# A spectral filter and an MLP on one core: one semaphore per loaded buffer, other first loads, and a new fixed order

## The chip, the core and the metric

The kernel runs on one core of a Trainium2 chip. The core has a matrix engine (TensorE, "PE" in the profile; its weight loads are "PEld"), VectorE (DVE), ScalarE (ACT), GpSimd (POOL) and SyncE (SP). SP, ACT and POOL also issue the DMA transfers; "SPq" in the profile is SyncE's issuing of them. The metric is the device time of one execution in microseconds (us). The kernel before takes 155.31 us, the median of three runs (154.14 to 155.58).

## What is computed

`x` is 2048 rows of 640, in bf16. Each row is normalised; the result goes through two branches, and both are added to `x`:

```python
xn = layernorm(x, axis=-1)
# branch A: a filter in the frequency domain
X  = rfft2(xn)                      # over the 2048 rows and the 640 columns
y  = irfft2(X * (w_r + 1j * w_i))   # filter: 2048 x 321, complex
# branch B: an MLP
h  = gelu(xn @ w1 + b1)             # 640 -> 1536
z  = h @ w2 + b2                    # 1536 -> 640
out = x + y + z
```

## The kernel before

**Tiles.** The 2048 rows are 16 tiles of 128 (row `16 p + c` is partition `p` of tile `c`), in eight pairs.

**Front.** VectorE takes the statistics of each tile (L574, L576, L578), GpSimd the inverse root (L580), and VectorE normalises (L598). Layer one of the MLP needs the tile transposed: tiles 0 to 7 by TensorE with an identity (L613) and a copy out of PSUM (L486 on ScalarE, L487 on VectorE), tiles 8 to 15 by DMA transposes from SyncE's queue (L603). For the filter, VectorE folds each pair four ways (L625, L629).

**Branch A** is a chain of matmuls with tables of sines and cosines. Group *a* (table `gtab`, one for each pair) transforms over the 128 rows; the result is cast into `XV`. Groups *b0* to *b5* (`etab`) transform over the columns into `Xb`, in matmuls of 160 columns. Groups *c00* to *c31* and *d00* to *d31* are small transforms of 32x32 matrices (`mtab`, `ntab`), 32 matmuls each. The first digit is one of four quarters (two pairs each), the second the half. Between *c* and *d*, VectorE multiplies by the filter (L730) and adds the products (L734). The casts after *d* write `U`. There are three slots of `U` for the eight pairs, lying in the tensors `gtab`, `T` and `U`. Each pair in `U` goes back into `XV` through two DMA transposes on SyncE's queue (L755), and its slot is free for another pair after them. Groups *e* (`getab`) and the last transform (`htab`) go back to 2048 x 640. Groups b, c, d and e all use PSUM banks 0 to 3, one group at a time.

**Branch B.** Layer one runs in blocks of 1, 1, 2, 2, 2, 4 and 4 tiles (matmuls of 128, 256 and 512 columns, five for each of 12 pieces of `w1`, into PSUM banks 4 to 7), and ScalarE applies the gelu (L663). Layer two is 12 pairs of matmuls (512+128 columns) for each tile. For eight "kept" tiles this runs early, and VectorE parks the sum with `b2` in SBUF (L829). For the other eight ScalarE copies the `b2` row into place (L808, from `b2bc`, the row spread over 128 partitions by a DMA), and layer two is summed in PSUM together with the `htab` matmul. GpSimd issues DMAs that add `x` to what is parked (L831), VectorE adds all (L840), SyncE stores (L843). While the first data are on their way, TensorE runs idle matmuls on zeros, 46 at the start and 12 after the first transposes (`WARM`).

**What sets the order.** Every instruction is recorded as an operation with what it reads and writes, a cost estimate and a priority. At build time `schedule` places the operations one by one on the engines by the estimates, and so fixes each engine's order and the buffers; `sync` then works out which waits are needed, and `emit` writes each engine's program in that order. The order of the groups b, c and d among themselves is given by `CHAIN`; `PRIO` gives priorities to kinds of operations; `HOLD` is how long TensorE prefers operations of the current tile mode. All matmuls are emitted on one line, L475, and all plain loads on L470, so the profile is read by tiles.

**Semaphores.** In `emit` each DMA has a semaphore of its own, and whoever needs it waits for the count 16. The filter is loaded by 34 DMAs, and the first L730 waits for all. Layer two waits for the two halves of `w2`. A cast into a `U` slot in its second or third use waits for the two transposes of the pair that used it before.

**First loads.** SyncE's queue issues `x` tile 0, the identity, `b1`, pieces 3 to 6 of `w1`, tiles 2 and 3, pieces 7 to 11, tiles 4 and 5, `gtab`, the other tiles in twos, the filter's first 16 loads, `w2`, the other 18 filter loads with the transposes of tiles 8 to 15 among them, `etab`, `mtab` and the `b2` row. ScalarE's queue issues tile 1 and pieces 0 to 2 of `w1`.

Of the kernel before, what the change touches and what calls it, by code (L numbers as in the profile page):

```python
# [13 lines left out]
D = 640  # L14
# [71 lines left out]
SWITCH = 0.095  # L86
HOLD = 0.1

# [68 lines left out]
class Sched:  # L157
# [5 lines left out]

    def op(self, engs, prio, emit, reads=(), writes=(), after=(), nbytes=0, gate=(), rate=330e3, alts=None, late=0.0, desc=128):
        o = Op()
        o.name = writes[0].name if writes else ""
        o.engs, o.prio, o.emit = engs, prio, emit
        o.reads, o.writes, o.after, o.gate = list(reads), list(writes), list(after), list(gate)
        o.nbytes, o.rate, o.late, o.desc = nbytes, rate, late, desc
        o.alts, o.alt = alts, None  # L170
        o.seq = len(self.ops)
        o.eng, o.done, o.inc, o.count, o.sem = None, False, False, None, None
        o.deps = [w for b in o.reads for w in b.writers] + list(after)
        for b in o.reads:
            b.readers.append(o)
        for b in o.writes:
            b.writers.append(o)
        self.ops.append(o)
        return o
# [13 lines left out]

    def schedule(self):
        free = {e: 0.75 for e in self.engines}
        dma_free = 0.0
# [102 lines left out]
    def sync(self):  # L299
        place = {o: (e, i) for e in self.engines for i, o in enumerate(self.order[e])}  # L300
        for o in self.ops:
            o.waits = [d for d in set(o.deps) if d.nbytes or d.eng != o.eng or o.eng != "pe"]
        pos = {e: 0 for e in self.engines}
        issued = set()
        know = {e: {} for e in self.engines}
        final = {}
        n = len(self.ops)
        while len(issued) < n:
            moved = False
            for e in self.engines:  # L310
                while pos[e] < len(self.order[e]):
                    o = self.order[e][pos[e]]
                    if any(d not in issued for d in o.waits):
                        break
                    k = know[e]
                    todo = []
                    for d in sorted(o.waits, key=lambda d: -d.start):
                        key, val = (("dma", d), 1) if d.nbytes else (d.eng, place[d][1])
                        if k.get(key, -1) >= val:
                            continue  # L320
                        todo.append(d)
                        for kk, vv in d.known.items():
                            if k.get(kk, -1) < vv:
                                k[kk] = vv
                        k[key] = max(k.get(key, -1), val)
                    final[o] = todo
                    for d in todo:
                        d.inc = True
                    o.known = dict(k)
                    issued.add(o)  # L330
                    pos[e] += 1
                    moved = True
            if not moved:
                raise RuntimeError("the order deadlocks")
        for o in self.ops:
            best = {}
            for d in final[o]:
                key = ("dma", d) if d.nbytes else d.eng
                if key not in best or place[d][1] > place[best[key]][1]:
                    best[key] = d  # L340
            o.waits = list(best.values())

    def emit(self, es, last):
        nc = self.nc
        sems = {e: nc.alloc_semaphore(f"s_{e}") for e in self.engines if e != "sp"}
        for e in self.engines:
            n = 0
            for o in self.order[e]:
                if o.nbytes:
                    o.sem, o.count = nc.alloc_semaphore(f"d_{o.seq}"), 16  # L350
                elif o.inc:
                    n += 1
                    o.sem, o.count = sems[e], n
# [21 lines left out]


BLOCKS = [(0, 1), (1, 1), (2, 2), (4, 2), (6, 2), (8, 4), (12, 4)]
W1P = [(0, 3), (3, 7), (7, 12)]
GROUPS = [(0, 2), (2, 3), (5, 3), (8, 3), (11, 3), (14, 2)]
BYDMA = tuple(range(8, 16))  # L380
ANY = [(0, 8)]
ZONE = {"hps": [(4, 8)], "bps": [(0, 4)], "cps": [(0, 4)], "dps": [(0, 4)],
        "eps": [(0, 4)], "fin": [(4, 8), (0, 4)], "fps": [(4, 8)], "tps": ANY, "aps": ANY}
PRIO = {"hps": 45, "gelu": 50, "pb": 70, "pc": 80, "filt": 85, "ipc": 90, "eps": 60, "fin": 40}
AHEAD = 2
CHAIN = "b0 b1 c00 c01 b2 c10 c11 d00 d01 b3 b4 c20 c21 d10 d11 b5 c30 c31 d20 d21 d30 d31".split()
XASPLIT = [((0, 1, 2, 3, 4),)] * 7 + [((0, 1), (2, 3, 4))]
KEEP = (1, 2, 4, 5, 7, 8, 10, 11)
HOME = (1, 2, 4, 5, 7, 8, 13, 14)
XO = ((0, 3, 6, 9, 12, 15, 1, 2), (4, 5), (7,), (8, 10, 11, 13, 14))  # L390
WARM = (46, 12)


def bass_parallel_sum__spectral_gfnet__dense_activation_gelu__prompt_kernel(
# [21 lines left out]
    with ExitStack() as es:  # L416
# [51 lines left out]

        def load(dst, src, buf, nbytes, after=(), reads=(), rate=360e3, q="sp", issue=0.45, late=0.0, desc=128):
            return K.op([(q, 1.0 if q == "pool" else issue)], 400, lambda e, _: e.dma_start(dst, src), reads=reads, writes=[buf], after=after, nbytes=nbytes, rate=rate, late=late, desc=desc)  # L470

# [38 lines left out]
        def load_x(c, n, q="sp"):  # L510
            o = load(view(X, c * D, [[1, n * D]]), xv[:, c:c + n, :].rearrange("p c d -> p (c d)"), B_x[c], n * D * 256, q=q, rate=375e3 if c else 300e3)
            for i in range(1, n):
                B_x[c + i].writers.append(o)
            return o
# [4 lines left out]
        load_x(0, 1)  # L519
        load_x(1, 1, "act")  # L520
        load_w1(0, "act")
        load(ident[:], const["I"], B_id, 32768, rate=150e3)
        load(b1t[:], b1v, B_b1, 3072)
        load_w1(1)
# [4 lines left out]
        for c in range(6, 16, 2):  # L529
            load_x(c, 2)  # L530
        WP = 32 * KP

        def load_w2(h):
            load(W2[:, 6 * h:6 * h + 6, :], w2v[:, 6 * h:6 * h + 6, :], B_w2, F * D, rate=390e3, desc=768)

        def load_w(wsrc, p0, off, row, n, step):
            up = step > 0 and n == 8
            load(bass.AP(tensor=Wf, offset=p0 * WP + off, ap=[[2 * WP, 16], [1, 8 * 321]] if up else [[2 * WP, 16], [321, n], [1, 321]]),
                 bass.AP(tensor=wsrc.tensor, offset=wsrc.offset + row * 321, ap=[[128 * 321, 16], [1, 8 * 321]] if up else [[128 * 321, 16], [step * 321, n], [1, 321]]),
                 B_w, 16 * 642 * n, rate=360e3 if up else 270e3, issue=0.45 if up else 0.645, desc=16 if up else 16 * n)  # L540
        rows = [(wsrc, 64 * qq + 32 * (lo ^ pp), 32 * qq + 16 * lo + 8 * pp, (16 * pp + 8 * ri) * 321)
# [12 lines left out]
        load(mtab[:], const["M"], B_m, 65536, rate=200e3)  # L554
        load(b2bc[:], bass.AP(tensor=b2v.tensor, offset=b2v.offset, ap=[[0, 128], [1, D]]), B_b2b, 163840)
        load(ntab[:], const["N"], B_n, 49152, rate=200e3)
# [5 lines left out]

        B_xnT = [Buf(f"xnT{c}") for c in range(16)]
        B_xa = [Buf(f"xa{c}") for c in range(8)]
        norm_ops, ring_ops, a_ops, TD = [], [], [], {}
# [17 lines left out]
        for pair in range(8):  # L583
# [10 lines left out]
            for n in range(2):  # L594
                c = 2 * pair + n
                pr = 100 - c / 2
                B_xn = Buf(f"xn_{c}")
                o = K.op([("dve", 0.356)], pr, lambda e, _, c=c, n=n, xnv=xnv: e.tensor_scalar(  # L598
                    out=xnv(n, 0, [[1, D]]), in0=view(X, c * D, [[1, D]]), scalar1=mv[:, c, 0:1], scalar2=rstd[:, c:c + 1], op0=ALU.subtract, op1=ALU.mult),
                    reads=[B_x[c], B_rs[c]], writes=[xn, B_xn])  # L600
                norm_ops.append(o)
# [5 lines left out]
                for j0, j1, engs in ((0, 3, ["dve"]), (3, 5, ["act"])) if c < 2 else ((0, 5, ["dve", "act"]),):  # L607
# [3 lines left out]
                    def xt(e, _, n=n, xnv=xnv, tps=tps, j0=j0, j1=j1):  # L611
                        for j in range(j0, j1):
                            ins = e.transpose(psb(tps.slot, [[1, 512]]).bitcast(BF)[:, 128 * j:128 * j + 128], xnv(n, 128 * j, [[1, 128]]), ident[:])  # L613
                        return ins
                    tp = K.op([("pe", nj * mm_us(128))], pr, xt, reads=[B_xn, xn, B_id], writes=[tps], alts=[[("128", nj * mm_us(128))]])
                    if j0 and not c:
# [4 lines left out]
                              lambda tps=tps, j0=j0, j1=j1: psb(tps.slot, [[1, 512]]).bitcast(BF)[:, 128 * j0:128 * j1].rearrange("p (j t) -> p j t", j=j1 - j0)),  # L621
                         reads=[tps], writes=[B_xnT[c]])
            pr = 100 - pair - 1.3
# [24 lines left out]
        for bi, (c0, nt) in enumerate(BLOCKS):  # L648
            for fc in range(NFC):
# [7 lines left out]
                for js in ((0, 1, 2), (3, 4)):  # L657
                    part_ = [pe([("128", len(js) * mm_us(128 * nt))], pr + 0.01 * len(part_), lambda c0=c0, nt=nt, fc=fc, hps=hps, js=js: [
                        (psb(hps.slot, [[1, 128 * nt]]), view(W1, F * j + 128 * fc, [[1, 128]]), xnT[:, c0:c0 + nt, j, :], j == 0, j == 4) for j in js],
                        reads=[B_w1s[w]] + B_xnT[c0:c0 + nt], writes=[hps], gate=part_)]  # L660
                    l1_ops += part_
# [36 lines left out]
        for P in range(4):  # L698
# [53 lines left out]
            for pair, U, B_u in zip(two, Us, B_us):  # L752
                for qq in range(2):
                    q = 2 * pair + qq
                    v_ops.append(K.op([("sp", 1.3)], 500, lambda e, _, q=q, qq=qq, U=U, uv=uv: e.dma_start_transpose(  # L755
                        XV[:, :, 128 * q:128 * q + 128], uv(U, D * qq, [[1, D]])), reads=[U, B_u], writes=[B_v[q]], nbytes=163840, rate=200e3))

# [126 lines left out]
```

## Time and profile before

| | |
|---|---|
| median of three runs | 155.31 us (154.14 to 155.58) |
| the profiled execution | 154.49 us |
| its span | 152.7 us |
| TensorE busy | 145.7 us (95%) |
| VectorE busy | 109.4 us (72%) |
| ScalarE busy | 81.2 us (53%) |
| granted TensorE clock | full throughout |

The span runs from the first to the last instruction that the profile shows; 1.8 us of the profiled execution lie around it. Ends of matmuls are modelled, so a busy TensorE can hide short stalls; where it matters, the spacing of starts is compared with the steady spacing of the same form. "Idle before" in a row is the time that the engine stood before these instructions, and the name behind the arrow is what ended most of it.

### The profile page before, as it was taken

The numbers are of one execution on the slowest core, as the hardware profiler recorded it, in microseconds if no ns is written. First come the engines' busy times: TensorE is split into PE (matmuls) and PEld (weight loads), VectorE is DVE, ScalarE is ACT, GpSimd is POOL, SyncE is SP. The second block draws the span as 40 slices with busy tenths as digits, with TensorE's granted clock in tenths as the row PEclk, the third lists the DMA queues.
The fourth block names the chain that finished last, engine by engine and source line by source line (L and its number), as shares of the span: only waits on it lengthen the run. The fifth ranks groups of instructions, "written<-read, shape, count | busy, mean of one in ns | idle before, by whom it ended". The sixth has DMA issues, their size and how long they took to land.

```text
span 152.7 us, 4239 instructions
## 1 busy us (share of the span) xinstructions
PE 145.7 (95%) x1796; PEld 94.3 (62%) x1796; DVE 109.4 (72%) x240; ACT 81.2 (53%) x149; POOL 21.1 (14%) x33
## 2 busy tenths in 40 slices
PE   7999899999979999799999999999999899999993
PEld 7988799988725545246544644454566555665563
DVE  0888999999933548899559979640198998787222
ACT  3197988889779765574634434746568200230000
POOL 1202110111206900200022002000334000000000
PEclk9999999999999999999999999999999999999999
DMA  4999999985688993125635273446294823311111
GB/s 144 284 401 404 318 280 384 214 154 124 160 141 250 234 258 91 24 69 39 133 75 105 65 98 82 107 90 124 50 203 106 210 86 133 129 43 43 54 73 50
DMA packets 29898, 23.02 MB, mean 151 GB/s; under 512 B 18104, under 2 KB 26424, under 8 KB 29880
## 3 DMA queue, kind: packets, MB, share of 16 engines
q1 hardware_dynamic: 26776, 16.86, 42.0%
q0 software_dynamic: 2304, 5.24, 15.4%
q10 hardware_dynamic: 800, 0.66, 1.3%
q8 instruction: 14, 0.23, 0.6%
q14 instruction: 4, 0.03, 0.1%
HBM read 13.58 MB, written 2.62 MB: 106 GB/s over the span
## 4 chain that ended last, share of the span: by engine, by line
PE 63%; DVE 22%; DMA 7%; SPq 2%; issue 2%; ACT 1%; DVEq 1%; POOL 1%
PE ps L475 63%; DVE stats L574 6%; DMA X<-in_A_x_dram 4%; DVE T L629 3%; DVE T L598 3%; DMA b2bc<-in_B_b_dram 2%; DVE T L625 2%; SPq L470 2%; DVE T L730 2%; DVE xnT L487 2%; DVE Z L734 1%; DVE mv L576 1%; DVE W L840 1%; DVEq L360 1%; POOL rstd L580 1%
## 5 line engine op out<-in xcount | busy, mean ns | idle before, releaser
L475 PE MATMUL ps<-xnT,W 128*128 128x256 bf16 (+2 forms) x420 | 57.4, 288 | 1.8 <-ACT gT L663 1.5
L475 PE MATMUL ps<-W,gT 128*128 128x512 bf16 (+3 forms) x396 | 57.9, 296 | 0.5 <-DVE W L840 0.5
L475 PEld LDWEIGHTS ps<-W,gT 128*128 128x128 bf16 x396 | 30.2, 98 | 24.3 <-issue 2.2
L475 PEld LDWEIGHTS ps<-xnT,W 128*128 128x128 bf16 x420 | 34.4, 98 | 17.3 <-ACT gT L663 3.6
L663 ACT ACTIVATE gT<-ps,b1col 128x256 bf16<-128x256 f32 (+2 forms) x84 | 38.8, 506 | 6.5 <-PE ps L475 5.6
L574 DVE BATCH_NORM_STATS2 stats<-X 128x6 f32<-128x320 bf16 x32 | 14.5, 476 | 3.3 <-DMA X<-in_A_x_dram 3.3
L486 ACT ACTIVATE Wf<-ps 128x960 bf16<-128x960 f32 (+1 forms) x8 | 6.7, 868 | 18.0 <-PE ps L475 18.0
L831 POOL DMA_DIRECT2D xnT<-in_A_x_dram x8 | 7.2, 932 | 56.0 <-DMA XV<-U 15.7
L730 DVE TENSOR_TENSOR T<-Y,Wf 128x1288 bf16<-128x1288 bf16 x16 | 12.4, 824 | 1.0 <-issue 1.0
L486 ACT ACTIVATE Xb<-ps 128x960 bf16<-128x960 f32 (+1 forms) x7 | 8.0, 1163 | 7.9 <-PE ps L475 7.9
L840 DVE TENSOR_TENSOR W<-ps,xnT 128x640 bf16<-128x640 f32 x8 | 6.5, 822 | 6.6 <-PE ps L475 6.6
L580 POOL TENSOR_TENSOR rstd<-ve,mhalf 128x2 f32<-128x2 f32 (+1 forms) x9 | 6.2, 693 | 33.5 <-DVE ve L578 33.5
L486 ACT ACTIVATE XV<-ps 128x1280 bf16<-128x1280 f32 (+1 forms) x8 | 9.5, 1184 | 2.5 <-PE ps L475 2.5
L487 DVE CAST Wf<-ps 128x960 bf16<-128x960 f32 (+1 forms) x4 | 4.3, 1073 | 8.4 <-PE ps L475 8.3
L487 DVE CAST Y<-ps 128x644 bf16<-128x644 f32 x8 | 6.6, 827 | 5.0 <-PE ps L475 5.0
L486 ACT ACTIVATE Y<-ps 128x644 bf16<-128x644 f32 x8 | 5.7, 707 | 7.5 <-PE ps L475 7.5
L831 POOL DMA_DIRECT2D X<-in_A_x_dram x8 | 8.2, 1436 | 6.6 <-DMA xnT<-T 6.6
L629 DVE TENSOR_TENSOR T<-T 128x512 bf16<-128x512 bf16 (+1 forms) x32 | 8.7, 318 | 0.0
L487 DVE CAST Xb<-ps 128x960 bf16<-128x960 f32 (+1 forms) x5 | 5.5, 1101 | 3.9 <-PE ps L475 3.9
L840 DVE TENSOR_TENSOR W<-ps,X 128x640 bf16<-128x640 f32 (+2 forms) x10 | 6.8, 687 | 2.1 <-PE ps L475 1.9
L486 ACT ACTIVATE U<-ps 128x512 bf16<-128x512 f32 (+1 forms) x14 | 5.4, 435 | 5.0 <-PE ps L475 5.0
L475 PE MATMUL ps<-getab,XV 32*128 32x160 bf16 (+1 forms) x128 | 7.6, 242 | 0.0
(47 smaller groups left out, 134.6 us busy)
## 6 DMA issues: line engine op xcount, KB each, us to landing
X<-in_A_x_dram POOLq DMA_DIRECT2D x8, 320.0 KB, 5.6
xnT<-in_A_x_dram POOLq DMA_DIRECT2D x8, 320.0 KB, 3.8
out_dram<-W SPq DMA_DIRECT2D x15, 160.0 KB, 1.8
X<-in_A_x_dram SPq DMA_DIRECT2D x7, 320.0 KB, 9.9
W<-in_B_w_dram SPq DMA_DIRECT2D x2, 960.0 KB, 8.2
Wf<-in_A_w_r_dram SPq DMA_DIRECT2D x15, 80.2 KB, 8.3
Wf<-in_A_w_i_dram SPq DMA_DIRECT2D x15, 80.2 KB, 5.3
W<-in_B_w_dram SPq DMA_DIRECT2D x1, 800.0 KB, 8.2
```

Source lines behind the costliest of these rows:

```text
L470: return K.op([(q, 1.0 if q == "pool" else issue)], 400, lambda e, _: e.dma_start(dst, src), reads=reads, writes=[buf], after=after, nbyte ...
L475: ins = e.matmul(o_, lhsT=lw, rhs=rh, start=st, stop=sp_, skip_group_check=True)
L486: return e.activation(dst(), src(), ACT.Copy, scale=scale)
L487: return e.tensor_copy(dst(), src())
L574: K.op([("dve", 0.393)], pr, lambda e, _, c=c, h=h: e.bn_stats(stats[:, c, 6 * h:6 * h + 6], view(X, c * D + H2 * h, [[1, H2]])), reads=[B ...
L580: K.op([("pool", 0.65)], pr, lambda e, _, a=a, b=b: e.tensor_tensor(out=rstd[:, a:b], in0=ve[:, a:b], in1=mhalf[:, a:b], op=ALU.pow), read ...
L598: o = K.op([("dve", 0.356)], pr, lambda e, _, c=c, n=n, xnv=xnv: e.tensor_scalar(out=xnv(n, 0, [[1, D]]), in0=view(X, c * D, [[1, D]]), sc ...
L629: ring_ops.append(K.op([("dve", dve_us(4 * w, 2))], pr, lambda e, _, op=op, x1v=x1v, xfv=xfv, o_=o_, o0=o0, o1=o1, w=w: e.tensor_tensor(ou ...
L663: K.op([("act", act_us(128 * nt, 1))], pr + PRIO["gelu"], lambda e, _, c0=c0, nt=nt, fc=fc, hps=hps: e.activation(gT[:, fc, 128 * c0:128 * ...
L730: filt_ops.append(K.op([("dve", dve_us(4 * KP, 2))], pr, lambda e, _, k=k, Y=Y, TB=TB, pair=pair: e.tensor_tensor(out=view(TT, TB.slot * 8 ...
L831: xo_ops[c] = K.op([("pool", 0.9)], 51 - c / 20, lambda e, _, c=c, xov=xov: e.dma_start(xov(0, D), xv[:, c, :], accum_op=ALU.add), reads=[ ...
L840: K.op([("dve", dve_us(w))], 95, lambda e, _, os_=os_, fps=fps, o0=o0, w=w, xov=xov, base=base: e.tensor_tensor(out=view(W1, OST + os_.slo ...
```

## The change

The change has these parts; lines are those of the changed file unless an old one is named.

1. **Semaphores.** Operations can be put into a group. The DMAs of a group share one semaphore, and whoever waits for one of them waits for the sum, 16 for each member: the 34 filter loads (544), the two halves of `w2` (32), and the DMA transposes into `XV` in four groups of four (64 each; one group is one quarter of branch A, two pairs). `schedule` still counts each DMA's own end as the time that a reader or a slot needs; the groups take effect in `sync` and `emit`.
2. **Loads.** ScalarE's queue issues the identity and then `w1`'s first piece; `w1` is cut 4+4+4 instead of 3+4+5. SyncE's queue issues tile 0, tile 1, `b1`, then `w1`'s second piece and the rest as before, with the `b2` row moved up behind the last tile of `x`, ahead of the filter.
3. **First tile.** Its normalisation is two instructions (384 and 256 columns), and the first three transposes and the first three matmuls of each piece of layer one wait for the first alone.
4. **Warm-up.** 43 and 5 idle matmuls instead of 46 and 12.
5. **Order.** Other priorities, `CHAIN`, `AHEAD` and `HOLD`, other cost estimates for some loads, and a table `NUDGE` that shifts the priorities of 87 single operations.

```diff
-HOLD = 0.1
+HOLD = 0.3
...
+        o.mates = [o] if grp is None else grp
+        if grp is not None:
+            grp.append(o)
...
+        for o in self.ops:
+            o.prio += 0 if o.nbytes and o.prio <= 450 else NUDGE.get(o.seq, 0)
...
-            o.waits = [d for d in set(o.deps) if d.nbytes or d.eng != o.eng or o.eng != "pe"]
+            o.waits = [m for d in set(o.deps) if d.nbytes or d.eng != o.eng or o.eng != "pe" for m in (d.mates if d.nbytes else [d])]
...
-                    o.sem, o.count = nc.alloc_semaphore(f"d_{o.seq}"), 16
+                    a = o.mates[0]
+                    if a.sem is None:
+                        a.sem = nc.alloc_semaphore(f"d_{a.seq}")
+                    o.sem, o.count = a.sem, 16 * len(o.mates)
...
-W1P = [(0, 3), (3, 7), (7, 12)]
+W1P = [(0, 4), (4, 8), (8, 12)]
...
-PRIO = {"hps": 45, "gelu": 50, "pb": 70, "pc": 80, "filt": 85, "ipc": 90, "eps": 60, "fin": 40}
-AHEAD = 2
-CHAIN = "b0 b1 c00 c01 b2 c10 c11 d00 d01 b3 b4 c20 c21 d10 d11 b5 c30 c31 d20 d21 d30 d31".split()
+PRIO = {'hps': 45, 'gelu': 35.4, 'pb': 125.8, 'pc': 115.0, 'filt': 114.9, 'ipc': 90, 'eps': 40.8, 'fin': 40.2}
+AHEAD = 4
+CHAIN = "b1 b0 c00 c01 b2 c11 d00 c10 b3 d01 b4 c21 c20 d11 d10 b5 c30 c31 d20 d21 d30 d31".split()
...
-WARM = (46, 12)
+WARM = (43, 5)
...
         load_x(0, 1)
-        load_x(1, 1, "act")
+        load(ident[:], const["I"], B_id, 32768, rate=150e3, q="act")
+        load_x(1, 1)
+        load(b1t[:], b1v, B_b1, 3072)
         load_w1(0, "act")
-        load(ident[:], const["I"], B_id, 32768, rate=150e3)
-        load(b1t[:], b1v, B_b1, 3072)
         load_w1(1)
...
         for c in range(6, 16, 2):
             load_x(c, 2)
+        load(b2bc[:], bass.AP(tensor=b2v.tensor, offset=b2v.offset, ap=[[0, 128], [1, D]]), B_b2b, 163840)
...
+        g_w, g_w2, g_v = [], [], [[] for _ in range(4)]
...
+                for d0, d1 in ((0, 384), (384, D)) if not c else ((0, D),):
...
-                        XV[:, :, 128 * q:128 * q + 128], uv(U, D * qq, [[1, D]])), reads=[U, B_u], writes=[B_v[q]], nbytes=163840, rate=200e3))
+                        XV[:, :, 128 * q:128 * q + 128], uv(U, D * qq, [[1, D]])), reads=[U, B_u], writes=[B_v[q]], nbytes=163840, rate=200e3, grp=g_v[q // 4]))
```

What this does to the programs of the engines, in so far as it is spoken of below:

- **TensorE.** All matmuls but the ten idle ones remain. Ahead of the first *b* group stand 24 pairs of layer two instead of 6, and 5 instead of 15 matmuls of 512 columns of layer one. The small groups follow the new `CHAIN`. Between *d21* and *d31* lie nine pairs of layer two, *d30*, three more pairs and 13 matmuls of 512 columns; between *d31* and the first *e* group 27 matmuls of 512 columns and nine pairs, where it was 33 and three.
- **ScalarE.** Six of the bias copies (old L808) move from behind the 256-column gelus of layer one: four stand among them and two right behind them. It copies the transposed tiles 3 and 7 out of PSUM, which VectorE did.
- **VectorE.** It casts one of the eight results of group *a* (1280 columns) in whole. Ahead of the first filter product stand waits for the filter (one, 544), four transposes of tiles and ScalarE. Its cast of *d30* into the `U` slot of pair 4 waits for the group of four transposes of the third quarter (64); before, this cast was ScalarE's, and waited for the two of pair 4.

## The prediction

> **What bounds the kernel now.** I read the busy shares first, then who waited for whom on TensorE, then the chain that ended last, then the timeline around each wait.
>
> The page's head, and TensorE's list of waits (total, times, longest, in us):
>
> ```profile
> span 152.7 us, 4239 instructions
> ...
> PE 145.7 (95%) x1796; PEld 94.3 (62%) x1796; DVE 109.4 (72%) x240; ACT 81.2 (53%) x149; POOL 21.1 (14%) x33
> ...
> PE ps L475 <- ACT gT L663: 1.5, 2, 1.1
> PE ps L475 <- DVE Y L487: 1.0, 1, 1.0
> ...
> PE ps L475 <- DVE W L840: 0.5, 1, 0.5
> ```
>
> TensorE is busy 95% of the span, so a new order can only win its stalls: some 7 us idle, of which about 1 lies at the start and 2.3 after the last matmul (it begins at 150.11). The three largest waits in between are 1.1 (at 44.26), 1.0 (at 64.06) and 0.5 us (at 121.77). The chain tells their causes (start, us, what):
>
> ```profile
> 39.38 3.49 DMA b2bc<-in_B_b_dram
> ...
> 42.90 0.74 ACT X L808
> 43.63 0.58 ACT gT L663
> ...
> 57.86 2.31 DVE T L730 x3
> 60.18 0.81 DVE Z L734 x2
> ...
> 63.27 0.75 DVE Y L487
> ```
>
> First: the bias row lands at 42.87, ScalarE stands before its copy L808, the gelu behind it is late, and TensorE waits 1.1. Second: ahead of the first filter product (L730) VectorE works through one wait for each of the 34 filter loads from 56.06 to 57.82. 0.8 of that lies beside the Y cast, 1.03 is idle, and the queue behind it (T, Z, xnT, Z, Y) hands it to TensorE at 64.06.
>
> **The change, part by part.** My unit is the steady spacing of matmuls: 512 columns 0.216 us, 256 columns 0.109, a pair 512+128 of W2 0.272 (24 matmuls in 3.26, from 139.50 to 142.76), one c or d group 0.44. All matmuls but ten warm-ups stay, so moving them alone costs nothing; I count waits.
>
> *One semaphore for the filter loads:* 34 waits become one, with four for transposes and one for ScalarE beside it. They fit under the 0.83 of the Y cast. **-1.1** (idle plus the modelled overlap of the matmul before); at worst 0, if something else then makes that Y late.
>
> *Bias row behind x:* the stall at 44.26 goes. TensorE also gets two whole kept tiles of W2 matmuls ahead of the b stage instead of half a tile, and ten fewer 512-column matmuls, so it has other work there. **-1.1**; at least -0.6, if ScalarE's casts of XV come out later.
>
> *ScalarE from 16.5 to 41.4.* What it did there:
>
> ```profile
> L663 ACT ACTIVATE gT<-ps,b1col 128x256 bf16<-128x256 f32 x36 | 15.1, 478 | 0.9
> L486 ACT ACTIVATE XV<-ps 128x1280 bf16<-128x1280 f32 x5 | 6.2, 1237 | 2.3 <-PE ps L475 2.3
> ```
>
> Its idle time there is 3.2 us (0.9+2.3). The new order puts four bias copies (0.67 each: three took 2.00 at 47.68) and a tile copy (estimate 0.6, the same 640 columns) into the stretch and hands one XV cast (1.13 from start to start) to VectorE: 2.7+0.6-1.1 = 2.2 more. It fits as a sum, not everywhere. The first copy needs the bias row, now behind the last x load, which was issued near 7.6 and landed 11.7 later, at 19.3; 164 KB at the 400 GB/s that the stretches from 9 to 17 us show put the row at 19.7. Copy and XV cast then hold ScalarE for 1.8 us while TensorE fills the four banks of the first layer in 4 x 0.547 = 2.2; the backlog meets the later copies with 0.25 to 0.9 us of stall. **+0.4**, from 0 up to +2.2 if all of it shows. VectorE's new XV cast lies beside 256-column work that TensorE has enough of.
>
> *First loads, first tile in two parts, W1 in equal parts, fewer warm-ups.* Tile 0 no longer shares its arrival with tile 1, three warm-ups fewer (0.11 each) and the half norm start the transposes some 0.3 earlier, and layer one need not wait for ScalarE's half copy. But the second part of W1 lands at 2.14+6.4 = 8.5, and TensorE stood before it until 8.71 already. It gets there with five more 128-column matmuls done (-0.28), while 160 KB more of W1 lie ahead (+0.4 at 400 GB/s); tiles 2 and 3 come as much later. The seven later warm-ups dropped (0.06 each) lay beside the copies they bridged. **+0.1** (-0.4 to +0.5).
>
> *The new order of the b, c and d groups.* For the first quarter I lay the rows end to end: c01, Y cast 0.63+0.83 later, three products 2.31, then the Xb cast of b2 (1.24) ahead of Z on VectorE, while TensorE has 1.63+1.27+1.46 up to c11: 0.4 late; d00 another 0.1. **+0.5** (0 to +0.8).
>
> *One semaphore for four transposes back into XV.* This is the part that I expect to cost. U has three slots for eight pairs: before, the second cast of d30, into the slot of pair 4, waits for the two transposes of pair 4. The timeline there (start, us):
>
> ```profile
> 94.87 0.77 ACT L486 ACTIVATE U<-ps 128x512 bf16<-128x512 f32 x2 [1.42 <-PE ps L475]
> ...
> 99.38 0.77 ACT L486 ACTIVATE U<-ps 128x512 bf16<-128x512 f32 x2
> ...
> 95.66 2.52 SPq L755 DMA_TRANSPOSE XV<-U  x2
> 98.22 2.60 SPq L755 DMA_TRANSPOSE XV<-gtab  x2
> DMA to landing us min/median/max: 2.4/2.7/4.5
> ```
>
> The cast began at 99.38, right as the gelu before it ended: the second transpose had landed 2.4 after its issue at 96.94. Now the same cast, on VectorE, waits for a count of 64, which is pair 5 too. From d21 on: its cast is done and SyncE starts 1.42 later (94.24 to 95.66); the fourth transpose is issued 3 x 1.28 after that and lands 2.4 to 2.7 later, at 7.7 to 8.0; the U cast takes 0.89, its semaphore 0.1; d31, which overwrites that PSUM, can start at 8.7 to 9.0. TensorE's queue from d21 to d31 is 0.44, nine pairs 2.45, d30 0.44, three pairs 0.82, 13 matmuls of 512 2.81: 6.96. So d31 waits 1.7 to 2.0, and TensorE, in order, with it. **+1.9** (0 to +2.2). With pair 4 alone it would be ready at 6.1 to 6.4, in time. What is behind d31 doesn't hide it: the inverse stage needs d31's four transposes, 7.7 to 8.0 later, and has 8.7 of matmuls meanwhile. Of what waits on VectorE behind the cast, all needs d31 anyway. The other two reuses wait for a group of four as well, but have 1.6 to 2 us to spare by the same sum, and the loads that add x to the output (L831) have more.
>
> The Trainium skill, "DMA: Bandwidth & Descriptors", section "Why a DMA increments its semaphore by 16 and not by 1", says that of two DMAs in flight on one semaphore only the full sum tells that data has landed, and advises one semaphore for each slot in flight: that speaks against just this part. The trace of before has no shared semaphore to show it; the price above is from rows alone.
>
> *Tail.* The wait of 0.5 at 121.77 (VectorE behind with L780 and L840) goes, and laying the new rows end to end leaves 0.5 in small pieces, the largest where the last tiles' PSUM is given back. **-0.1** (-0.5 to +0.5).
>
> **Sum:** -1.1 -1.1 +0.4 +0.1 +0.5 +1.9 -0.1 = **+0.6**. The profiled execution took 154.49 us (152.7 and 1.8 around it), below the median of the runs, 155.31; the four known executions average 154.88. Added to that: **155.5**.
>
> **Rivals.**
> 1. *The group wait is covered.* If d21 comes early enough, or ScalarE's casts and the transposes run closer than 1.28 apart, d31 finds its PSUM free. For it: 1.9 is a difference of two long sums, each of nine rows. Against: no row shows a faster spacing. With the c11 and ScalarE stalls away too, 155.5-1.9-0.5-0.4 = 152.7.
> 2. *ScalarE becomes the bound from 17 to 41 us: the other side.* It decides if what is added (2.2 us) and the time it stands before the bias row exceed the idle 3.2, that is, if the row lands over 1 us after ScalarE gets there, at about 20.6. For it: the row took 3.49 us to land before, against 2.7 for the larger etab. Against: two transposes were issued beside it then, from 39.86 on. All of the 2.2 then shows: 155.5+1.8 = 157.3.
> 3. *The change doesn't remove the filter waits' cost*, since the transposes' semaphores, still waited for there, are late: term one is 0, 156.6. Against: the last of them was issued near 44, 12 us ahead.
>
> **How the numbers follow.** Forecast 0.38 (own range 154 to 156.8), rival one 0.30, two 0.28, three 0.04. About 1% (1.55 us on 155.31) is what a measurement of this kernel tells from no change: faster is below 153.8, rival one; slower above 156.9, rival two; forecast and rival three are the same. Range 152.4 to 157.5, a little beyond rivals one and two, with the bounds of the tail and the first loads.
>
> **What would show it.** TensorE waits about 1.9 us for a VectorE cast of U with 27 matmuls of 512 columns of layer one still to come, and VectorE for a transpose. No bias wait of over 1 us near 43, no idle ahead of the first T. In 17 to 28 us TensorE waits for gelus below 1 us in all. I am wrong if d31 starts under 8 us after d21, or if TensorE stands in the first 40 us for 2 us more than before.

## Result and profile after

The changed kernel takes **154.09 us**, the median of 20 executions (152.75 to 156.72); the kernel before took 155.40 beside it (20 executions, 154.14 to 157.86). The ratio is **0.990** (95% interval 0.988 to 0.993): 1% faster, some 1.3 us. The ratios in this document leave out executions more than 1.5% above the fastest of their kernel; the medians do not, and where the difference matters (the granted TensorE clock was below 1.0 in some executions) the text says so. Forecast was 155.5, no change; the time lies in the range, but it moved the other way.

The profiled execution took 154.80 us, with a span of 153.0. The head of its page and its line of granted clock:

```profile
span 153.0 us, 4203 instructions
...
PE 146.2 (96%) x1786; PEld 94.0 (61%) x1786; DVE 109.3 (71%) x236; ACT 81.3 (53%) x154; POOL 21.0 (14%) x33
...
PEclk9999999999999999999999999996999999999999
```

Ten idle matmuls fewer, and one slice, from 103 to 107 us, in which TensorE was granted less than its full clock; before had none. Who waited for whom (total, times, longest, in us), from the list of all engines:

```profile
DVE U L501 <- DMA XV<-gtab: 3.7, 1, 3.7
...
PE ps L489 <- DVE U L501: 2.7, 1, 2.7
...
ACT X L831 <- DMA b2bc<-in_B_b_dram: 0.8, 1, 0.8
```

The waits of 1.1 at 44.26, 1.0 at 64.06 and 0.5 at 121.77 are gone. In their place stands one of 2.7, for the U cast that waits for a transpose. The chain that ended last (start, us, what):

```profile
7.34 11.40 DMA b2bc<-in_B_b_dram
...
18.83 0.74 ACT X L831
19.57 1.12 ACT XV L500
20.69 0.37 ACT gT L686
...
21.11 2.14 PE ps L489 x18
...
101.24 2.65 DMA XV<-gtab
...
103.91 0.90 DVE U L501 x2
...
104.85 22.56 PE ps L489 x198
```

It has just two places where something other than TensorE sets the time: the bias row near 19 us, which costs TensorE 0.33 at 21.11, and the U cast ahead of d31.

To see where TensorE gained and lost, I subtracted from the start of a group the sum of all useful matmuls queued ahead of it, at the steady spacing of the prediction (idle matmuls count as nothing). The rest is what TensorE had lost by then:

| lost by the start of | before | after | difference in the stage |
|---|---|---|---|
| the first b group | 47.87 - 38.38 = 9.49 | 48.12 - 41.12 = 7.00 | -2.49 |
| d21 | 94.24 - 82.19 = 12.05 | 94.89 - 86.24 = 8.65 | -0.91 |
| d31 | 100.76 - 88.49 = 12.27 | 104.85 - 93.20 = 11.65 | +2.78 |
| the first e group | 109.16 - 96.88 = 12.28 | 114.94 - 101.92 = 13.02 | +1.36 |
| the last e group | 134.78 - 121.50 = 13.28 | 139.95 - 126.40 = 13.55 | -0.47 |

The sum is +0.27, and the spans differ by +0.3. So these two profiles lie 0.3 apart, not far from the forecast 0.6, but through other terms, and neither is typical: before's is 0.9 below its median, after's 0.7 above. The experiments had to say why.

### The profile page after: what moved, and what is told of

It reads as the page before. It is cut to its first block, busy times and chain, and to the rows that moved or that the text cites. A ratio compares the mean times of both kernels' runs of the same rounds, so it can differ in the third digit from the quotient of the medians.

```text
span 153.0 us, 4203 instructions
## 1 busy us (share of the span) xinstructions
PE 146.2 (96%) x1786; PEld 94.0 (61%) x1786; DVE 109.3 (71%) x236; ACT 81.3 (53%) x154; POOL 21.0 (14%) x33
## 4 chain that ended last, share of the span: by engine, by line
PE 82%; DMA 9%; SPq 4%; ACT 2%; DVE 1%; issue 1%; ACTq 0%
PE ps L489 81%; DMA b2bc<-in_B_b_dram 7%; SPq L484 4%; DMA XV<-gtab 2%; ACT XV L500 1%; ACT gT L686 1%; DVE U L501 1%; ACT X L831 0%; PE ps L633 0%; DVE W L863 0%; SPq L778 0%; ACTq L368 0%
## 5 line engine op out<-in xcount | busy, mean ns | idle before, releaser
L489 PE MATMUL ps<-xnT,W 128*128 128x256 bf16 (+2 forms) x420 | 58.2, 291 | 0.6 <-ACT gT L686 0.3
L854 POOL DMA_DIRECT2D xnT<-in_A_x_dram x8 | 9.4, 1405 | 55.6 <-DMA XV<-gtab 25.1
L501 DVE CAST Wf<-ps 128x960 bf16<-128x960 f32 (+1 forms) x5 | 5.1, 1021 | 9.7 <-PE ps L489 9.6
L500 ACT ACTIVATE Xb<-ps 128x960 bf16<-128x960 f32 (+1 forms) x6 | 6.8, 1139 | 9.0 <-PE ps L489 9.0
L501 DVE CAST Y<-ps 128x644 bf16<-128x644 f32 x7 | 5.8, 827 | 6.7 <-PE ps L489 6.7
L854 POOL DMA_DIRECT2D X<-in_A_x_dram x8 | 9.3, 2095 | 7.9 <-DMA xnT<-T 7.9
L500 ACT ACTIVATE XV<-ps 128x1280 bf16<-128x1280 f32 (+2 forms) x8 | 8.7, 1100 | 2.8 <-PE ps L489 2.7
L501 DVE CAST Xb<-ps 128x960 bf16<-128x960 f32 (+1 forms) x6 | 6.7, 1122 | 4.3 <-PE ps L489 4.3
L803 DVE TENSOR_TENSOR Wf<-Wf 128x960 bf16<-128x960 bf16 (+1 forms) x12 | 7.0, 594 | 1.0 <-ACT Wf L500 0.8
L852 DVE TENSOR_TENSOR xnT<-ps,b2bc 128x640 f32<-128x640 f32 x6 | 4.9, 819 | 3.7 <-PE ps L489 3.6
```

Of the source, the lines that this page charges most:

```text
L489: ins = e.matmul(o_, lhsT=lw, rhs=rh, start=st, stop=sp_, skip_group_check=True)
L500: return e.activation(dst(), src(), ACT.Copy, scale=scale)
L501: return e.tensor_copy(dst(), src())
L803: K.op([("dve", dve_us(320 * n, 2))], pr + 2, lambda e, _, k=k, op=op, yo=yo, y2=y2, n=n: e.tensor_tensor(out=view(Wf, Y2 + y2.slot * 3 * ...
L854: xo_ops[c] = K.op([("pool", 0.9)], 51 - c / 20, lambda e, _, c=c, xov=xov: e.dma_start(xov(0, D), xv[:, c, :], accum_op=ALU.add), reads=[ ...
```

## Experiments

Except where an instruction is moved or added on purpose, each edit keeps every engine's instruction order, so that only the wait or the load named differs. They were done in three lots, each on one chip, with before run beside them: its medians were 155.60, 157.09 and 155.26 (43 executions, 153.66 to 158.94).

### Semaphores by pair

```diff
-        g_w, g_w2, g_v = [], [], [[] for _ in range(4)]
+        g_w, g_w2, g_v = [], [], [[] for _ in range(8)]
...
-                        ... grp=g_v[q // 4]))
+                        ... grp=g_v[q // 2]))
```

> The changed kernel, its order kept on every engine, but the transposes back into XV share a semaphore by pair (count 32) and no longer by quarter (64). Theory A: the 2.73 us that d31 stood in the profile of after is the group wait and nothing else. With pair 4 alone its second transpose is issued near 97.6 and lands 2.5 to 3.1 later, the U cast of 0.89 ends by 101.6, and TensorE gets to d31 at 102.1: no wait, granted clock 1.0 throughout, 2.6 us less than the executions of after at full clock (about 153.2), so 150.6, or 0.969 of before. Rival: what comes behind d31 (its transposes, the inverse stage, the final sums) is as late as before and takes the gain back: 152.5 to 153.5, with a new wait ahead of the first e group or in the tail.

Measured: 152.05 us (151.26 to 154.17), ratio 0.982 (0.972 to 0.991), granted clock 0.999 or 1.0 in all six executions. It ran once more in the last lot:

> The changed kernel with semaphores by pair once more, on the chip of the old order with the filter group, to price the new order (parts 1 to 4 are the same in both but for the two-part first tile). If the new order is worth what its ledger shows (0.3 at d00 and 0.4 to 0.8 at d31 lost, 0.5 won in the last tiles, no bias copies late), it is within 0.6 of that kernel: 151.3 to 152.1. Rival: the new order is worth 1 us or more either way.

Measured: 151.59 (150.53 to 152.07), ratio 0.977 (0.972 to 0.982). So sharing by pair is worth 2.0 to 2.5 us over sharing by quarter by the medians, and 1.3 to 1.7 against the executions of after at full clock (median 153.31). The rival (all given back behind d31) is out, but theory A's 150.6 was not reached either. It named no wait at all; one is left. The timeline of after, and then of the kernel by pair:

```profile
94.89 0.51 PE L489 MATMUL ps<-Z,ntab 32*32 32x320 bf16 x32
...
96.31 2.52 SPq L778 DMA_TRANSPOSE XV<-U  x2
...
98.87 3.65 SPq L778 DMA_TRANSPOSE XV<-gtab  x2
...
103.91 0.89 DVE L501 CAST U<-ps 128x512 bf16<-128x512 f32 x2 [3.72 <-DMA XV<-gtab]
...
104.85 0.77 PE L489 MATMUL ps<-Z,ntab 32*32 32x320 bf16 x32 [2.73 <-DVE U L501]
```

```profile
96.81 2.52 SPq L778 DMA_TRANSPOSE XV<-U  x2
...
102.50 0.89 DVE L501 CAST U<-ps 128x512 bf16<-128x512 f32 x2 [1.82 <-DMA XV<-U]
103.45 0.52 PE L489 MATMUL ps<-Z,ntab 32*32 32x320 bf16 x32 [0.82 <-DVE U L501]
```

By quarter the cast waits for the second transpose of `gtab`, pair 5; by pair for that of `U`, pair 4, and TensorE stands 0.82 instead of 2.73. The rest comes from that transpose: issued 1.26 after 96.81, it landed 4.4 later; the row that the prediction used had 2.4. Why it was late, the profile does not show.

### d31 later

```diff
+        pe_, d31 = K.order["pe"], zone["d31"]
+        k = pe_.index(d31)
+        pe_[k:k + 3] = pe_[k + 1:k + 3] + [d31]
         K.sync()
```

> The changed kernel with semaphores by pair, and d31 behind five more matmuls of 512 columns of layer one (1.08 us), where by pair it still stood 0.4 to 0.8 for the U cast whose transpose landed 4.4 us after its issue. Theory A: the wait goes and e0 does not wait, since 22 matmuls of 512 columns and nine pairs (4.75 and 2.45) follow d31 and its four transposes take 7.7 to 8.0 in the prediction's sum, so at most 0.6 shows there: 0.2 to 0.7 faster than by pair. Rival: the whole gain is given back at e0, within 0.2 of the kernel by pair.

Measured: 151.92 (151.56 to 153.55), ratio 0.981 (0.976 to 0.987), no faster than by pair (151.59 in the same lot). The rival holds, but at another place than it named:

```profile
103.24 0.51 PE L489 MATMUL ps<-Z,ntab 32*32 32x320 bf16 x32
...
103.86 0.77 ACT L500 ACTIVATE T<-ps 128x512 bf16<-128x512 f32 x2 [1.55 <-PE ps L489]
...
104.51 1.27 ACT L686 ACTIVATE gT<-ps,b1col 128x512 bf16<-128x512 f32 x2
...
105.25 4.49 PE L489 MATMUL ps<-xnT,W 128*128 128x512 bf16 x20 [0.97 <-ACT gT L686]
```

d31 itself waits for nothing. But ScalarE's cast of its result stays ahead of two gelus in ScalarE's queue and now comes later; TensorE stands 0.97 for the gelu. A step moved on one engine needs its consumers moved too.

### A quarter's semaphore in the old order

```diff
-                        ... nbytes=163840, rate=200e3))
+                        ... nbytes=163840, rate=200e3, grp=g_v[q // 4]))
```

> The kernel before, its order kept, with one semaphore for the four transposes of a quarter back into XV (64) and nothing else. Theory A: the second U cast of d30 (ScalarE, at 99.38 before) now waits for the fourth transpose, issued at 99.5 and landing 2.4 to 3.6 later, so it ends at 102.8 to 103.9 and d31 starts 2.1 to 3.2 later than at 100.76: 2.1 to 3.2 us slower than before, ratio 1.014 to 1.020, and some executions with a lower granted clock. Rival: the wait lies in slack (d31 is followed by 33 matmuls of 512 columns that need nothing of it): within 0.5 of before.

Measured: 160.35 (158.24 to 161.82), ratio 1.026 (1.019 to 1.034), granted clock below 0.99 in four of five executions. TensorE's waits in its profile, an execution at full clock:

```profile
PE ps L481 <- ACT gT L670: 2.6, 2, 2.1
PE ps L481 <- ACT U L492: 2.2, 1, 2.2
PE ps L481 <- DVE Y L493: 1.0, 1, 1.0
```

The second line is the group wait: 2.2 at d31, as theory A had it; the median shows over 3 us with the lost clock, and the ratio is above the 1.014 to 1.020 expected. So the cost is the group's, not the new order's. The first line was not expected: the wait at the gelu behind the bias row is 2.1 here and was 1.1 in the profile of before, though up to some 70 us, where the first transposes back into XV are issued, both kernels are the same program. SyncE's and ScalarE's timeline of this kernel:

```profile
19.88 7.91 SPq L476 DMA_DIRECT2D Wf<-in_A_w_r_dram  x9
...
40.89 0.43 SPq L476 DMA_DIRECT2D b2bc<-in_B_b_dram  x1
...
44.27 0.74 ACT L815 ACTIVATE X<-b2bc 128x640 f32<-128x640 bf16 x1 [2.85 <-DMA b2bc<-in_B_b_dram]
```

SyncE came to the row at 40.89 and not at 39.38. Most of that arose far ahead of it: SyncE spent 7.91 us on issuing nine filter loads, where the profile of before has

```profile
20.13 6.47 SPq L470 DMA_DIRECT2D Wf<-in_A_w_r_dram  x9
```

and the transposes and loads behind them went out later. The row landed 1.4 later, and so did the first b group (49.25 against 47.87). **The stall of 1.1 that the prediction priced is that of one execution, and the smaller of the two seen.**

### The bias row and the first loads, alone and together

```diff
+        sp = K.order["sp"]
+        sp.remove(B_b2b.writers[0])
+        sp.insert(sp.index(B_x[14].writers[0]) + 1, B_b2b.writers[0])
         K.sync()
```

> The kernel before, its order kept, with the load of the bias row issued right behind the last load of x instead of behind mtab; nothing else. The prediction and theory C both expect that the wait of 1.1 us at 44.26 goes and nothing takes its place: 1.0 to 1.3 us faster, ratio 0.992 to 0.994. Rival: the 164 KB that now lie ahead of the filter and the transposes of tiles 8 to 15 delay layer one of these tiles (blocks of four) or VectorE's first product: 0 to 0.6 faster.

Measured: 152.97 (152.57 to 153.28), ratio **0.975** (0.970 to 0.981). Of TensorE's two waits for gelus in before (1.5 us in all, the longest 1.1) one of 0.5 is left in its profile:

```profile
PE ps L475 <- ACT gT L663: 0.5, 1, 0.5
```

```diff
+W1CUT = [(0, 4), (4, 8), (8, 12)]
...
+        sp, act = K.order["sp"], K.order["act"]
+        x1, idl = B_x[1].writers[0], B_id.writers[0]
+        act.remove(x1)
+        sp.remove(idl)
+        act.insert(act.index(B_w1s[0].writers[0]), idl)
+        sp.insert(sp.index(B_b1.writers[0]), x1)
+        x1.eng, idl.eng = "sp", "act"
```

The loads and the waits for `w1` go by the new cut, and 43 and 5 idle matmuls are issued; the rest stays.

> The kernel before, its order kept, with only the first loads of the change: w1 cut 4+4+4, tile 1 from SyncE's queue, the identity from ScalarE's, 43 and 5 idle matmuls (the first tile stays in one part). Theory C: the front gains 1 to 1.5 us up to 18 us (the first matmul of 256 columns at 16.3 to 16.8 instead of 17.82), but the bias row still lands near 42.9, since the loads ahead of it set that, so the wait for the gelu behind it grows from 1.1 to 2 to 2.5 us and the time stays within 0.5 of before: the two parts only pay together. Rival (terms that add): 1.2 to 1.5 us faster than before, ratio 0.991.

Measured: 154.70 (154.49 to 156.52), ratio 0.989 (0.982 to 0.996). That is the number of the rival, not of theory C.

> The kernel before, its order kept, with both: the first loads of the change and the bias row behind the last load of x. Theory C: the front's gain now reaches the b stage, 2.3 to 2.8 us faster than before (ratio 0.982 to 0.985), more than the two alone add up to; the first b group starts at 45.2 to 45.6 (47.87 before). Rival: the gain of the front is taken by the next late load (the transposes of tiles 8 to 15, etab), so that it is no faster than with the bias row alone, 0.992 to 0.994, and the first b group starts at 46.7.

Measured: 152.19 (151.88 to 152.67), ratio **0.971** (0.966 to 0.976).

Theory C says that the front pays only once the row is early. By the medians of this lot it pays alone, too (154.70 against 157.09). Profile against profile the theory holds: the first b group starts at 47.87 before, 47.86 with the front alone (TensorE's largest wait grows from 1.1 to 1.4), 46.78 with the row alone, 45.94 with both. The gain of 0.8 that the front has with the row early is nothing without it in these profiles, since the row's landing sets when TensorE goes on. So the tie between the two parts is shown for these four executions; why the median with the front alone fell all the same stays open.

By medians all three gained some 2 to 3 us more than expected. What differs is not these kernels but before: in that lot it took 155.57 to 158.60, the kernel with nothing but the row early 152.57 to 153.28. With the row early, a late SyncE queue does no harm: in that profile SyncE is done with `mtab` at 41.07, where the profile of before was at 39.33, yet TensorE's longest wait ahead of the b stage, once its first data are there, is 0.5.

### The bias row still later

```diff
+        sp, row = K.order["sp"], B_b2b.writers[0]
+        k = sp.index(row)
+        sp[k:k + 3] = sp[k + 1:k + 3] + [row]
         K.sync()
```

> The kernel before, its order kept, with the load of the bias row issued behind two more transposes (2.54 us of SyncE's issuing). Theory D: an execution's time hangs on how late the row lands, and the granted clock on how long TensorE then stands. The row lands near 45.5 to 47, TensorE stands 3.5 to 5 us at the gelu behind it, nearly all executions have a mean granted clock of 0.989 or below (4 of the 9 last executions of before had), and the time is 3 to 5 us over that of before. Rival: the clock has nothing to do with the gap: 2.5 us slower, and half of the executions at 1.0.

Measured: 160.53 (158.52 to 162.09), ratio 1.023 (1.016 to 1.031). All six executions had a granted clock of 0.989 (three) or 0.979 (three). TensorE's timeline and, below it, the view by windows (window, its length, TensorE busy, weight loads, VectorE, ScalarE, GpSimd, then the granted clock, DMA share and GB/s):

```profile
42.93 1.24 PE L475 MATMUL ps<-xnT,W 128*128 128x512 bf16 x5
49.94 2.31 PE L475 MATMUL ps<-xnT,W 128*128 128x512 bf16 x5 [5.78 <-ACT gT L663]
```

```profile
46.00:48.00 2.00, 0.00 (x0) 0.00 (x0) 0.00 (x0) 0.00 (x0) 0.00 (x0) 1.00 0.49 124
48.00:50.00 2.00, 0.06 (x1) 0.06 (x2) 0.00 (x0) 1.42 (x3) 0.00 (x0) 0.50 0.90 158
50.00:52.00 2.00, 2.00 (x5) 0.67 (x6) 0.00 (x0) 2.00 (x3) 1.04 (x1) 0.50 0.89 266
52.00:54.00 2.00, 1.78 (x13) 1.48 (x13) 0.64 (x1) 1.55 (x3) 0.88 (x1) 0.50 0.91 253
54.00:56.00 2.00, 2.00 (x16) 1.28 (x15) 0.05 (x1) 2.00 (x4) 0.91 (x2) 0.79 0.78 172
```

TensorE stood 5.78 us, the clock was halved from 48 to about 55 us, and five matmuls of 512 columns took 2.31 instead of 1.24. Theory D holds: here TensorE stood long enough for the clock to go too, and the row's lateness set both. The sizes are larger than expected, since the two transposes ahead of the row took SyncE 3.69 us instead of 2.54 and the row landed at 48.5.

### Idle matmuls in the gap

```diff
+        nxt = next(o for o in pe_[pe_.index(d31):] if o.name.startswith("hps") and o in l1_ops and l1_ops.index(o) % 2 == 0)
+        gap = K.op([("pe", 2.2)], 0, mms(lambda: [(psb(nxt.writes[0].slot, [[1, 128]]), warm[:], warm[:], True, True) for _ in range(40)]))
...
+        pe_.insert(pe_.index(d31), gap)
         K.sync()
```

> The changed kernel as it is, with 40 idle matmuls of 128 columns (2.24 us at the spacing of 0.056) in TensorE's queue right ahead of d31, where it stood 2.73 us; they write a PSUM bank that the next piece of layer one overwrites. Theory B: the lower granted clock that 7 of 20 executions of after showed (0.989 in the mean, 0.86 from 105 to 115 us) follows from that gap, at a cost of 1.4 us; filled, all executions have 1.0, d31 still starts at about 104.8, and the median is that of the executions of after at full clock, 153.2 (0.985 of before). Rival: the clock has nothing to do with the gap, or the idle matmuls delay d31: 154.1 to 154.5, with a third of the executions at 0.989.

Measured: 153.55 (152.87 to 154.94), ratio 0.993 (0.989 to 0.998); the granted clock was 0.999 or 1.0 in all twelve executions. (Of the 20 of after, eight were at 0.989 or 0.988, not seven as the expectation counted: their median is 154.96, that of the other twelve 153.31.) d31 still started 9.7 us after d21. So filling the gap keeps the clock and nothing else, and the median is that of the executions of after at full clock within 0.3. Eight of 20 against none of twelve is some evidence by itself; with the two kernels above (all of six and four of five low where TensorE stands longer; none of 30 by pair, with 34 waits or with the old front, where it stands less) I take the cause as shown.

### The first loads in the new order

```diff
 W1P = [(0, 4), (4, 8), (8, 12)]
...
+W1CUT = [(0, 3), (3, 7), (7, 12)]
...
+        act.insert(act.index(B_w1s[0].writers[0]), x1)
+        sp.insert(sp.index(B_b1.writers[0]), idl)
+        x1.eng, idl.eng = "act", "sp"
```

> The kernel with semaphores by pair, with the first loads as before: w1 cut 3+4+5, tile 1 from ScalarE's queue, the identity from SyncE's, 46 and 12 idle matmuls; the first tile stays in two parts, and the order of all other instructions is kept. Theory A: the front is what the prediction sized wrongly; the first matmul of 256 columns began at 15.79 in after and at 17.82 in before, so this kernel is 1.5 to 2.0 us slower than the kernel by pair. Rival (the prediction's own term of +0.1, -0.4 to +0.5): it differs by no more than 0.5, and the 2 us come from the new order in 13 to 18 us.

Measured: 153.56 (153.06 to 155.09), ratio 0.991 (0.987 to 0.996), 1.5 us over the kernel by pair in the same lot. TensorE's wait list has the reason:

```profile
PE ps L490 <- DMA W<-in_B_w_dram: 1.8, 2, 1.4
```

It stood 0.44 before the second part of `w1` and 1.36 before the third, which is five pieces by the old cut and four by the new; by pair the waits for `w1` were 0.5 in all. Theory A's size is right. Its two starts were not: 15.79 and 17.82 are those of rows that lump 128- and 256-column matmuls together. Taken instruction by instruction from the traces, the first matmul of 256 columns starts at 14.91 in after and at 16.73 in before, and the last gelu of 128 columns ends at 16.13 and at 17.42: 1.8 and 1.3 gained by then.

### The 34 waits

```diff
-                 B_w, ..., desc=16 if up else 16 * n, grp=g_w)
+                 B_w, ..., desc=16 if up else 16 * n)
```

> The kernel with semaphores by pair, and each of the 34 filter loads with its own semaphore again; order kept. Theory A: the waits cost VectorE what they cost before (1.76 us from 56.06 to 57.82, 0.8 of it beside a Y cast), the Z before d00 has no slack (TensorE lost 0.4 there in after), so 0.9 to 1.1 us slower than the kernel by pair, seen as a wait at d00. Rival: in the new order ScalarE and TensorE have enough else there and the waits lie in idle time of VectorE: within 0.3 of the kernel by pair.

Measured: 152.09 (151.82 to 152.43), ratio 0.983 (0.977 to 0.988), the same as by pair, as the rival had it. Yet the wait is there, one group earlier than either theory placed it:

```profile
57.53 2.31 DVE L753 TENSOR_TENSOR T<-Y,Wf 128x1288 bf16<-128x1288 bf16 x3 [1.03 <-issue]
...
61.05 0.50 PE L489 MATMUL ps<-Xb,mtab 32*32 32x322 bf16 x32 [1.03 <-DVE Xb L501]
```

VectorE's 1.03 of idle ahead of T goes through to c11. But then TensorE came later to d00 and d31 and stood 0.2 and 0.4 less there (0.44 instead of 0.82 at d31). Half of it was slack ahead of a later wait; the other half is within what these medians can tell.

### The old order with loads and filter group

Before with the new first loads, the early row and one semaphore for the 34 filter loads:

> The kernel before in its own order, with the new first loads, the bias row behind the last load of x, and one semaphore for the 34 filter loads; transposes keep a semaphore each, the old table of priorities stays. It is the kernel with front and bias row, less the stall of 1.04 at c11 that all profiles of the old order show. The prediction's term (-1.1) and theory A expect 151.0 to 151.3 (the kernel with front and bias row had 152.19), no wait at c11; then it is as fast as the changed order with semaphores by pair or faster by up to 1 us, and the new order by itself gives nothing. Rival: VectorE's queue behind the Y cast (T, Z, Xb, Z) is late at the next group instead and gives back half or more: 151.7 to 152.2.

Measured: 151.48 (151.02 to 151.57), ratio 0.976 (0.972 to 0.980). The stall at c11 is gone (its start is 61.08, 1.61 after c10; it was 2.71). The median lies between the two expectations. It is 0.7 below that of the kernel without the group, but that one ran in another lot, and the ratios to before (0.971 and 0.976) do not show the gain; that the stall is gone is shown by the profiles. By pair in the new order took 151.59 in the same lot. **The table of 87 shifted priorities, the new chain and the other costs are worth nothing that this can measure**, and these two kernels, the fastest of the study, beat both the kernel before and the changed one.

## Why the prediction was wrong

Medians of the kernels that add one part at a time, against the prediction's terms. They come from different lots; the kernel by pair, run in two of them, differs by 0.5, and before by 1.8. So a single step is less certain than the sum: against before of its own lot (157.09) the first step is -4.1.

| added | median, us | step | predicted |
|---|---|---|---|
| before | 155.40 | | |
| bias row behind x | 152.97 | -2.4 | -1.1 |
| first loads | 152.19 | -0.8 | +0.1 |
| one semaphore for the filter | 151.48 | -0.7 | -1.1 |
| new order, first tile in two, by pair | 151.59 to 152.05 | +0.1 to +0.6 | +0.8 (0.4 + 0.5 - 0.1) |
| transposes by quarter (after) | 154.09 | +2.0 to +2.5 | +1.9 |
| sum | | -1.3 | +0.6 |

- **Bias row: "-1.1; at least -0.6". This is the step that failed most.** The mechanism was right; the term was mis-sized: it measured -2.4 or more by the medians. Its size was read from one execution. The wait is not a fixed 1.1 but hangs on how far SyncE has come by then: 1.1 and 2.1 in two profiles of the same program; and where TensorE stood much longer, 5.78 us, the clock was lost on top. I also added "the four known executions average 154.88" as if all terms had been measured in an average execution; the profiled one was near the fastest.
- **First loads: "+0.1".** This term failed next: it measured -0.8 in the old order and -1.5 in the new. I sized them from the one wait that showed, and added late arrivals of tiles 2 and 3, which did not come. By the ledger front and ScalarE together gained some 1.4 by the first b group, beside the 1.1 of the row. I also missed the tie between two parts that the profiles show: with the row late, the first b group starts no earlier (47.86 against 47.87).
- **One semaphore for four transposes: "+1.9 (0 to +2.2)".** Right as a mechanism, at the place, for the cast and with the 27 matmuls named; from d21 to d31 it was 9.96 and not 8.7 to 9.0. The second `gtab` transpose was issued at 101.24, 4.93 after the first of the four and not 3.84; SyncE's issuing of the two for `gtab` took 3.65 (3.74 and 3.66 in the two profiles by pair) and not 2.60 as in the old order; why stays open. So the stand of 2.73 was itself beyond the bound of 2.2, and the clock came on top: +1.36 more in the stage behind it. In the old order the wait was 2.2. The Trainium skill, "DMA: Bandwidth & Descriptors", section "Why a DMA increments its semaphore by 16 and not by 1", advises one semaphore for each slot in flight, for the correctness of the data and not for time. The runs here fit it in time as well: a slot here is a pair, and by pair the kernel takes 2.0 to 2.5 us less.
- **Filter waits: "-1.1".** -0.7 by medians of two lots in the old order, 1.1 at c11 by the profiles; in the new order about half is taken back by later waits.
- **ScalarE: "+0.4".** TensorE waited 0.33 at 21.11, behind copy and XV cast as described; the row landed at 18.74, earlier than the 19.7 that I reckoned. Rival two is out.
- **New order: "+0.5", tail "-0.1".** c11 did not wait, d00 lost 0.4; the tail gained 0.5. Small, and right in the sum.

Neither sign that I had named for being wrong came (d31 under 8 us after d21, or 2 us more of standing in the first 40 us): the error lay in what was gained. Rival one, group wait covered, gave 152.7; the time lies halfway between it and the forecast, and for another reason, since the group wait was there in full.

## What to carry to other kernels

A wait for a transfer, read from one profile, is a sample: compare the profiled time with the spread of the runs, and see what queue the transfer was issued from, before pricing it. A gain ahead of a late arrival can be lost in the wait for it, as in the profile with the front alone: look whether that arrival moves too. Share a semaphore only among transfers that one consumer waits for anyway (34 filter loads, a pair), not across buffers that come free at different times.

## What the runs showed of the hardware

The granted clock was not expected to play a part. In after it halved 2.3 us into a stand of 2.73 us (from 102.12 to 104.85; windows as above):

```profile
102.00:104.00 2.00, 0.13 (x1) 0.00 (x0) 0.09 (x1) 0.20 (x1) 0.00 (x0) 1.00 0.41 82
104.00:105.00 1.00, 0.15 (x16) 0.15 (x32) 0.80 (x2) 0.00 (x0) 0.00 (x0) 0.71 0.00 0
105.00:106.00 1.00, 1.00 (x34) 0.24 (x20) 0.27 (x1) 0.28 (x1) 0.00 (x0) 0.50 0.00 0
...
107.00:108.00 1.00, 1.00 (x5) 0.34 (x3) 0.00 (x0) 0.31 (x1) 0.00 (x0) 0.58 0.27 54
108.00:110.00 2.00, 2.00 (x11) 0.94 (x10) 0.00 (x0) 1.23 (x2) 0.00 (x0) 1.00 0.70 137
```

It stayed at half for some 3.4 us (0.58, 2 and 0.84 in the windows from 104 to 108). With the row still later it halved some 3.9 us into the stand of 5.78. The means of the executions come in steps, 1.0, 0.989 and 0.979: at half clock, 0.011 and 0.021 of some 155 and 160 us are 3.4 and 6.7 us, one stretch and two. One costs about 1.65 us here (154.96 against 153.31). Stands of 1.1 to 2.2 us showed no loss in the profiles; one of 2.73 did, and eight of the 20 executions of that kernel had the lower mean; 5.78 us lost two stretches.

The Trainium skill, "TensorE: Matmul & The Clock Gate", Part 1, says that the clock falls to half after an idle window of about 3.4 us, that the window runs freely, so that the moment varies between runs, and that the clock is either half or full (it names a third value for three busy cores of a die). The half agrees with these runs, the 3.4 us with how long each loss lasted, and the varying moment with the 2.3 and 3.9 us. That a whole idle window is needed, and the advice in its section "Why this matters for your kernels" to keep gaps below about 3 us, do not: 2.73 us were enough.

Open remain the executions of before at a low clock (10 of 43): none was profiled, so that it is the bias row which takes the clock there is concluded from the kernels of the old order with the row earlier (none of 16) and later (all of 6), not seen; the front alone, with the row late, had none of 5. Nor does the clock explain most of the spread of before: its other 33 executions, at 0.999 or 1.0, run from 153.66 to 158.94. That the row's landing sets this spread is concluded from the 1.1 and 2.1 above and from the 152.57 to 153.28 with the row early; no slow execution of before was profiled.
